# A long convolution beside an FFN in one instruction stream: the second stage's products back come after the next group's spectra, the last stage takes the second half first, and the stages' weights and the casts' places change

## The chip, the cores and the metric

The kernel runs on one core of one Trainium2 chip. The metric is device time of one execution in microseconds. Engines are named as in the profile: PE (matmuls), PEld (its weight loads), DVE, ACT, POOL, and SP, which only issues DMAs; a q behind a name is that engine's instruction queue.

## What is computed

x = A_q has 2048 rows of 576. The output is a sum of three terms:

```python
xn = _layernorm(x, axis=-1)
return x + _A_ref(xn, A_k, A_v, ...) + _B_ref(xn, B_w1, B_w2)
...
# _B_ref: the FFN
h = jnp.maximum(jnp.einsum("bsd,df->bsf", x, w1), 0)
return jnp.einsum("bsf,fd->bsd", h, w2)      # d = 576, f = 4608
...
# _A_ref: q = xn, a short causal convolution of k (4 taps), times v,
# then a causal convolution over all 2048 rows per channel with ssm_k (by FFT),
# plus kv * ssm_D, and a gate with q
return q * y
```

All is float32. The kernel splits operands into a high and a low part of 12 bits each (type fp32r) and multiplies hi x hi, hi x lo and lo x hi.

## The kernel before, in words

**The FFN.** x stands in 16 row tiles of 128 (T = 16), in four blocks b of four tiles. A first half of the work takes blocks 0 and 1 through all of w1 and w2, a second half blocks 2 and 3. w1 and w2 are cut into 12 chunks of 384 columns (three column tiles j), so the chunk index ci runs from 0 to 23. `mm1` (L304) makes one column tile of the hidden layer for a block: 14 matmuls of 512 columns into a PSUM tile psh (two buffers), then ACT makes hh (relu) and DVE ll (the rest). `mm2` (L323) makes one row tile's sum in two halves h of 288 columns: nine matmuls each into pso (three buffers), then DVE adds it to acc, times rstd (L337). `drain` places the mm2 of the last block between the mm1 of the next. Per block that is 42 matmuls of L314 and 72 of L334.

**Weights.** `load_w1` and `load_w2` bring a chunk on SP (one buffer each, r1 and r2). `split_w1` and `split_w2` cast a column tile to hi on ACT (L289, L297) and POOL subtracts for lo (L262). SPLITS says behind which mm1 each stands.

**Layer norm.** `stats` gives mean and variance on DVE, `inv_std` 1/sqrt through ACT's square root. `first_xT` and `make_xT` (L237) centre x, transpose it on PE and split it. They only centre; rstd multiplies at the accumulation, which is allowed since relu commutes with a positive factor. Block 2 and 3 are prepared while chunk 11 runs, in place (L745).

**The convolution** is a generator, `conv` (L379), that yields after each small step. It goes through: loading kt = ssm_k (16 DMAs of small pieces, L392), the first transform of k (wk, 128 matmuls), that of the gated convolution of k and v, called x here (wx, 128 matmuls, with DVE's taps L454 to L463), the second stage (L504 on: 32 groups g, 6 steps and 18 matmuls each) and the last stage (L592 on: 16 tiles t with two units u of two halves; 64 steps of two matmuls, then gate and sum on DVE). Between stages the data goes through DRAM (zk, zx, zy).

**How the two are interleaved.** `tick` (L685) is called twice per mm1 and twice per mm2 with the columns done; it adds `rate` times that to an account, and when the account is not negative it takes one step of the generator and subtracts that step's weight (W_FK, W_FX, W_FM, W_FO, L53). So a larger weight spreads a stage over more of the FFN. A negative yield is a pause in FFN columns. The rate comes from SHARE, the part of the FFN in which the stream is to end. In the last chunk of each half, `mm2` calls `rest_of_stream` at each tile t >= HT = 8 (L342), which takes all steps that are left, because the last sum of those tiles (acc) must contain the convolution. Tiles below 8 were stored to fin in DRAM after the first half, and the last stage reads them back (ft) and stores the result from POOL's queue.

The program is then ordered by the scheduler of the tile framework, which moves an instruction ahead when it expects it to be ready; `tc.issue_after(ins)` keeps instructions behind ins on its engine. So the order on an engine is not the order of the code.

Of the kernel before, what the change touches and what calls it, by code (L numbers as in the profile page):

```python
# [10 lines left out]
F32 = mybir.dt.float32  # L11
# [29 lines left out]
N_WARM = 22  # L41

# [6 lines left out]
SHARE = 0.95  # L49
# [3 lines left out]
W_FK, W_FX, W_FM, W_FO = 1.6, 3.7, 1.8, 2.1  # L53
# [54 lines left out]
def h3_ffn_kernel(ctx: ExitStack, tc, x, k, v, shift_k, ssm_k, ssm_D, w1, w2, fwd, inv, mid, out):  # L108
# [100 lines left out]
    def first_xT(srcs):  # L209
# [7 lines left out]
        for t in range(BT):  # L217
# [3 lines left out]
            with tc.issue_after(behind.ins) if behind else nullcontext():  # L221
                stats(t, srcs[t])
                if t % 2 == 0:
                    behind = nc.vector.tensor_scalar(neg[:, t:t + 1], mv[:, t, 0:1], -1.0, None,
                                                     op0=OP.mult)
                    nc.scalar.activation(xn, srcs[t], AF.Identity, bias=neg[:, t:t + 1])
                else:
                    behind = centred(xn, srcs[t], t)
            for c in range(5):
                w = min(P, D - c * P)  # L230
                nc.tensor.transpose(ps[c][:w, t * P:(t + 1) * P], xn[:, c * P:c * P + w], ident)
        for c in range(5):
            split_x(0, c, ps[c])
# [3 lines left out]
    def make_xT(b, srcs, in_place=False):  # L237
# [3 lines left out]
        with tc.issue_after(done["dve"].ins):  # L241
# [4 lines left out]
        for t in range(t0, t0 + BT):  # L246
# [6 lines left out]
            centred(xn[-1], srcs[t], t)  # L253
        for c in range(5):
# [4 lines left out]
            split_x(b, c, ps)  # L259

# [23 lines left out]
    def split_w1(ci, j):  # L284
# [4 lines left out]
        nc.scalar.activation(h1, r1[:, :, cols], AF.Copy)  # L289
# [3 lines left out]
    def split_w2(ci, j):  # L293
# [3 lines left out]
        nc.scalar.activation(h2, r2[:, j, :], AF.Copy)  # L297
# [4 lines left out]
    hid = {}  # L302

# [19 lines left out]
    def mm2(ci, b, i):  # L323
        t = b * BT + i
        cols = slice(i * P, (i + 1) * P)
        for h in range(2):
# [3 lines left out]
            for j in range(FT):  # L330
# [6 lines left out]
            done["acc"] = nc.vector.scalar_tensor_tensor(  # L337
                acc[t][:, dc], ps[:, :NH], rstd[:, t:t + 1], acc[t][:, dc],
                op0=OP.mult, op1=OP.add)
            tick(W_MM2 / 2)  # L340
        if ci % NCHUNK == NCHUNK - 1:
            if t >= HT:  # L342
                rest_of_stream()
# [3 lines left out]
            else:  # L347
                if t >= T - 2:
                    move(acc[t], out, t, store=True)
                elif t % 2:  # L350
# [28 lines left out]
    def conv():  # L379
# [124 lines left out]
        with tc.tile_pool(name="fm", bufs=2) as fp:  # L504
# [38 lines left out]
            pend = None  # L543
            for g in range(NG + 1):
                yy = None
# [3 lines left out]
                if pend is not None:  # L549
                    yh = fp.tile([P, D], F32R, tag="yh", name=f"yh{g - 1}")  # L550
                    yl = fp.tile([P, D], F32R, tag="yl", name=f"yl{g - 1}")
                    yy = yh, yl
                for h in range(2):
# [6 lines left out]
                    if pend is not None:  # L560
                        if h == 0:
                            p1, p2 = pend
                            nc.vector.tensor_tensor(p1, p1, p2, OP.add)
                            nc.scalar.activation(yh, p1, AF.Copy)
                        else:
                            nc.vector.tensor_tensor(yl, p1, yh, OP.subtract)
                    yield W_FM
                if yy is not None:
                    vo = fp.tile([P, D], F32, tag="vo", name=f"vo{g - 1}")
                for h, (name, z) in enumerate((("k", zk), ("x", zx))):  # L570
                    if yy is not None:
                        ps, cols = run(*yy, 1, h)
                        nc.scalar.activation(vo[:, cols], ps, AF.Copy)
                    split(name, g + 1)
                    load(z, g + 2, name)
                    yield W_FM
                if yy is not None:
                    nc.sync.dma_start(rows(zy, g - 1), vo)
                if g < NG:
                    sw = fp.tile([P, D], F32, tag="sw", name=f"sw{g}", bufs=1)  # L580
                    for h in range(2):
# [4 lines left out]
                        if h == 1:  # L586
                            nc.vector.tensor_tensor(k2, sw, k2, OP.mult)
                        yield W_FM
                    pend = k1, k2


        with tc.tile_pool(name="fo", bufs=2) as fp:  # L592
            raw, parts, rest, ys = {}, {}, {}, {}

            def load_z(t, u):
                if t < T:
                    raw[t, u] = fp.tile([P, D], F32, tag="zt", name=f"zo{t}_{u}", bufs=4)
                    nc.sync.dma_start(raw[t, u], zy[:, T * u + t, :])

            def load_rest(t):  # L600
                if t < T:
# [8 lines left out]
                    rest[t] = w, xt, ft  # L610

            def split(t, u):
                if t < T:
                    hi = fp.tile([P, D], F32R, tag="hi", name=f"ohi{t}_{u}", bufs=3)
                    lo = fp.tile([P, D], F32R, tag="lo", name=f"olo{t}_{u}", bufs=3)
                    with here():
                        nc.scalar.activation(hi, raw[t, u], AF.Copy)
                        nc.vector.tensor_tensor(lo, raw[t, u], hi, OP.subtract)
                    parts[t, u] = hi, lo

            def gate(t):

                if t >= 0:
                    with here():
                        nc.vector.scalar_tensor_tensor(ys[t], rest[t][1], mv[:, t, 0:1], ys[t],
                                                       op0=OP.subtract, op1=OP.mult)

            def add(t):
                if t >= 0:
                    to, more = (ys[t], rest[t][2]) if t < HT else (acc[t], acc[t])  # L630
                    with here():
                        nc.vector.scalar_tensor_tensor(to, ys[t], rstd[:, t:t + 1], more,
                                                       op0=OP.mult, op1=OP.add)
                    if t < HT:
                        move(to, out, t, store=True, queues=(nc.gpsimd, nc.gpsimd))

            units = [(t, u) for t in range(T) for u in range(U)]
            for n in range(3):
                load_z(*units[n])
            for t in range(2):  # L640
# [158 lines left out]
```

## Time and profile before

| | us |
|---|---|
| runs, median of 3 (lowest to highest) | 1116.33 (1114.97 to 1117.08) |
| the profiled execution | 1114.96 |
| its span, first to last instruction | 1113.2 |
| PE, DVE, ACT, POOL busy in it | 1080.5, 737.3, 583.5, 265.4 |

How to read the rows that follow: a group's row has line, engine, operation, out<-in, shapes and count, then busy time in us and mean ns of one, then the engine's idle time just before these instructions and what ended most of it. A timeline row has start and length in us, and in brackets the idle time before it. Busy time on PE counts from a matmul's start to its modelled end, and matmuls overlap; what they really take is seen from start to start.

### The profile page before, as it was taken

What the parts mean: (1) busy time and instruction counts of PE and PEld (TensorE: products, weight loads), DVE (VectorE), ACT (ScalarE), POOL (GpSimd) and SP (SyncE); (2) the same over time, 40 slices, a digit from 0 to 9 for tenths busy, and PEclk for the clock granted to TensorE, in tenths of its full rate; (3) what the DMA queues carried; (4) which work ended last, traced back from release to release, by engine and by line L of the source; (5) the groups of instructions that cost most, each with busy time, mean ns of one, the idle gap of its engine ahead of it and who ended that gap; (6) DMA issues with size and microseconds to landing.
All of it is one profiled execution on the core that took longest, in us unless ns stands there. A gap on an engine that the chain in (4) does not pass through costs nothing.

```text
span 1113.2 us, 17349 instructions
## 1 busy us (share of the span) xinstructions
PE 1080.5 (97%) x6534; PEld 980.5 (88%) x6534; DVE 737.3 (66%) x1215; ACT 583.5 (52%) x1180; POOL 265.4 (24%) x215
## 2 busy tenths in 40 slices
PE   8999999999999999999999999999999999998698
PEld 5889999988898988999989999999999999997587
DVE  6353876759999999358555654655555655468985
ACT  4221778713433343357566665676656666545540
POOL 3230331412412313303121131220312302214200
PEclk9999999999999999999999999999999999999699
DMA  9940464664544533426544133342342412288823
GB/s 236 175 144 1 145 192 138 191 184 140 178 145 152 180 118 130 142 75 201 175 132 132 54 122 99 96 121 64 121 123 63 131 54 90 89 247 248 232 73 86
DMA packets 112640, 150.79 MB, mean 135 GB/s; under 512 B 45229, under 2 KB 63279, under 8 KB 112556
## 3 DMA queue, kind: packets, MB, share of 16 engines
q1 hardware_dynamic: 104572, 135.98, 41.2%
q0 software_dynamic: 7824, 13.11, 4.5%
q8 instruction: 51, 0.84, 0.3%
q10 hardware_dynamic: 160, 0.59, 0.2%
q14 instruction: 33, 0.27, 0.1%
HBM read 114.26 MB, written 35.39 MB: 134 GB/s over the span
## 4 chain that ended last, share of the span: by engine, by line
PE 69%; DVE 16%; DMA 6%; issue 4%; ACT 3%; SPq 1%; POOL 1%; DVEq 0%; ACTq 0%; POOLq 0%
PE pso L334 30%; PE psh L314 29%; PE psf L533 6%; DVE e L457 4%; DVE acc L337 3%; DVE c L458 3%; DMA r<-in_w 2%; PE psf L369 2%; DVE ll L320 1%; DVE xs L363 1%; DVE c L454 1%; SPq L392 1%; DVE c L463 1%; DMA k-1_2411<-in_k 1%; POOL l L262 1%
## 5 line engine op out<-in xcount | busy, mean ns | idle before, releaser
L262 POOL TENSOR_TENSOR l<-r,h 128x640 fp32r<-128x640 f32 (+1 forms) x144 | 229.5, 1609 | 646.6 <-ACT h L297 318.7
L334 PE MATMUL pso<-h,hh 128*128 128x288 f32 x1152 | 339.0, 296 | 7.9 <-DVE acc L337 7.6
L334 PE MATMUL pso<-l,hh 128*128 128x288 f32 x1152 | 339.2, 295 | 0.0
L334 PE MATMUL pso<-h,ll 128*128 128x288 f32 x1152 | 338.9, 295 | 0.0
L337 DVE SCALAR_TENSOR_TENSOR acc<-pso,rstd,acc 128x288 f32<-128x288 f32 x384 | 193.4, 512 | 90.1 <-PE pso L334 88.3
L334 PEld LDWEIGHTS pso<-h,hh 128*128 128x128 f32 x1152 | 216.3, 188 | 17.4 <-DVE acc L337 11.3
L314 PE MATMUL psh<-xhi,h 128*128 128x512 f32 x576 | 226.7, 394 | 1.5 <-DVE ll L320 1.1
L314 PE MATMUL psh<-xlo,h 128*128 128x512 f32 x576 | 226.2, 393 | 0.0
L314 PE MATMUL psh<-xhi,l 128*128 128x512 f32 x576 | 225.6, 392 | 0.0
L334 PEld LDWEIGHTS pso<-l,hh 128*128 128x128 f32 x1152 | 216.8, 188 | 5.3
L334 PEld LDWEIGHTS pso<-h,ll 128*128 128x128 f32 x1152 | 216.7, 188 | 0.7
L320 DVE SCALAR_TENSOR_TENSOR ll<-psh,hh 128x512 fp32r<-128x512 f32 x144 | 98.6, 686 | 123.2 <-ACT hh L319 122.9
L319 ACT ACTIVATE hh<-psh 128x512 fp32r<-128x512 f32 x144 | 85.1, 593 | 141.4 <-PE psh L314 139.8
L314 PEld LDWEIGHTS psh<-xhi,l 128*128 128x128 f32 x576 | 108.5, 188 | 21.7
L314 PEld LDWEIGHTS psh<-xhi,h 128*128 128x128 f32 x576 | 108.3, 188 | 18.4 <-DVE ll L320 1.6
L314 PEld LDWEIGHTS psh<-xlo,h 128*128 128x128 f32 x576 | 108.5, 188 | 15.9 <-DVE xlo L203 0.4
L289 ACT ACTIVATE h<-r 128x640 fp32r<-128x640 f32 x72 | 52.4, 734 | 62.8 <-PE psh L314 30.4
L297 ACT ACTIVATE h<-r 128x576 fp32r<-128x576 f32 x72 | 46.9, 678 | 52.7 <-DMA r<-in_w 29.1
L585 DVE TENSOR_TENSOR k<-psf,k 128x288 f32<-128x288 f32 x64 | 29.1, 455 | 66.8 <-ACT sw L584 66.6
L583 ACT ACTIVATE sw<-psf 64x288 f32<-64x288 f32 x64 | 26.1, 408 | 88.9 <-PE psf L533 87.7
L314 PE MATMUL psh<-xhl,l 128*128 128x512 f32 x144 | 56.5, 392 | 0.0
L314 PE MATMUL psh<-xhl,h 128*128 128x512 f32 x144 | 56.2, 391 | 0.0
(104 smaller groups left out, 1414.3 us busy)
## 6 DMA issues: line engine op xcount, KB each, us to landing
r<-in_w SPq DMA_DIRECT2D x24, 864.0 KB, 6.6
r<-in_w SPq DMA_DIRECT2D x23, 768.0 KB, 5.6
zk<-zk SPq DMA_DIRECT2D x32, 288.0 KB, 2.4
zx<-zx SPq DMA_DIRECT2D x32, 288.0 KB, 2.4
ztk<-zk SPq DMA_DIRECT2D x32, 288.0 KB, 2.8
ztx<-zx SPq DMA_DIRECT2D x32, 288.0 KB, 2.8
zy<-vo SPq DMA_DIRECT2D x32, 288.0 KB, 2.2
zo<-zy SPq DMA_DIRECT2D x32, 288.0 KB, 3.5
```

Source lines behind the costliest of these rows:

```text
L262: return nc.gpsimd.tensor_tensor(dst, src, hi, OP.subtract)
L289: nc.scalar.activation(h1, r1[:, :, cols], AF.Copy)
L297: nc.scalar.activation(h2, r2[:, j, :], AF.Copy)
L314: nc.tensor.matmul(ps, a, m, start=i == 0, stop=i == len(seq) - 1)
L319: done["act"] = nc.scalar.activation(hh, ps, AF.Relu)
L320: nc.vector.scalar_tensor_tensor(ll, ps, 0.0, hh, op0=OP.max, op1=OP.subtract)
L334: nc.tensor.matmul(ps[:, :NH], a[:, cols], m[:, dc], start=n == 0, stop=n == 3 * FT - 1)
L337: done["acc"] = nc.vector.scalar_tensor_tensor(acc[t][:, dc], ps[:, :NH], rstd[:, t:t + 1], acc[t][:, dc], op0=OP.mult, op1=OP.add)
L457: nc.vector.tensor_tensor(e, win[t - n], sk[:, n, :], OP.mult)
L458: nc.vector.tensor_tensor(sums[t], sums[t], e, OP.add)
L533: nc.tensor.matmul(ps[:, :NH], a, m[:, cols], start=n == 0, stop=n == 2)
L585: nc.vector.tensor_tensor(k1[:, cols], ps, k1[:, cols], OP.mult)
```

## The change

- Second stage: in a group the steps of x's spectrum come right behind those of k's. The matmuls back of the group before (run(*back, 1, h)) come last. The sum k1 + k2 and its cast yh are made at the end of their own group, yl at the start of the next one.
- Last stage: tiles 8 to 15 first, then 0 to 7. `rest_of_stream` is no longer called in `mm2`; instead the last chunk's mm2 of tile t takes steps until t is in `added`.
- Stage weights and SHARE are new.
- `make_xT` multiplies by rstd (normalized), so for blocks 1 to 3 DVE's accumulation is a plain add; block 0 keeps the old form. For blocks 2 and 3 the statistics stand behind the last acc instead of the last split of x.
- `at_turn`: from chunk 1 on, the casts of weights on ACT stand behind the last hh.
- Start: tile 3 is centred on ACT too; 6, 3 and 2 more warm matmuls after the transposes of tiles 1, 2 and 3; the warm matmuls write a psh tile; the casts of chunk 0's w1 tiles 1 and 2 stand behind the centring and behind the split of x.
- End: the last tile's store goes out by halves, one part on SP, one on ACT.

```diff
-SHARE = 0.95
+SHARE = 0.985
-W_FK, W_FX, W_FM, W_FO = 1.6, 3.7, 1.8, 2.1
+W_FK, W_FX, W_FM, W_FO = 1.4, 4.1, 1.26, 2.4
...
+            keep_warm(WARM_TILE[t])
+        with tc.issue_after(done["act"].ins):
+            split_w1(0, 1)
...
-        with tc.issue_after(done["dve"].ins):
+        with tc.issue_after(done["acc" if in_place else "dve"].ins):
...
-            centred(xn[-1], srcs[t], t)
+            normalized(xn[-1], srcs[t], t)
...
+    def at_turn(ci):
+        return tc.issue_after(done["act"].ins) if ci else nullcontext()
...
+        if ci == HALVES * NCHUNK - 1:
+            while t not in added:
+                next(stream)
...
+            if b == 0:
+                done["acc"] = nc.vector.scalar_tensor_tensor(
+                    acc[t][:, dc], ps[:, :NH], rstd[:, t:t + 1], acc[t][:, dc],
+                    op0=OP.mult, op1=OP.add)
+            else:
+                done["acc"] = nc.vector.tensor_tensor(acc[t][:, dc], ps[:, :NH], acc[t][:, dc],
+                                                      OP.add)
+            if ci == HALVES * NCHUNK - 1 and t == T - 1:
+                for u, queue in ((0, nc.sync), (1, nc.scalar)):
+                    queue.dma_start(out[u, :, t, dc], acc[t][halves(u)[0], dc])
             tick(W_MM2 / 2)
         if ci % NCHUNK == NCHUNK - 1:
-            if t >= HT:
-                rest_of_stream()
...
+                    for h in range(2):
+                        ps, cols = run(*parts["x", g], 0, h)
+                        nc.scalar.activation(sw[:64, cols], ps[64:], AF.Copy)
+                        nc.scalar.activation(sw[64:, cols], ps[:64], AF.Copy)
+                        nc.vector.tensor_tensor(k1[:, cols], ps, k1[:, cols], OP.mult)
+                        if h == 0:
+                            split("k", g + 1)
+                            load(zk, g + 2, "k")
+                        yield W_FM
...
+                    if back is not None:
+                        ps, cols = run(*back, 1, h)
+                        nc.scalar.activation(vo[:, cols], ps, AF.Copy)
+                    if g < NG:
+                        if h == 0:
+                            nc.vector.tensor_tensor(k2, sw, k2, OP.mult)
+                            split("x", g + 1)
+                            load(zx, g + 2, "x")
+                        else:
+                            nc.vector.tensor_tensor(k1, k1, k2, OP.add)
+                            yh = fp.tile([P, D], F32R, tag="yh", name=f"yh{g}")
+                            nc.scalar.activation(yh, k1, AF.Copy)
+                            pend = yh, k1
...
+            order = [*range(HT, T), *range(HT)]
+            units = [(t, u) for t in order for u in range(U)]
```

Three places in the built program show what moved. In names, the numbers behind a tile's name are chunk, block or tile, and tile half; the last is the buffer's own.

PE in the last stage of the kernel before; ohi and olo are the two parts of a unit's input (tile and unit in the name):

```order
L657 MATMUL psf_10856<-ohi7_0_10788,wi7_10655 128x288
L658 MATMUL psf_10856<-olo7_0_10789,wi7_10655 128x288
L657 MATMUL psf_10894<-ohi7_1_10843,wi7_10655 128x288
L658 MATMUL psf_10894<-olo7_1_10844,wi7_10655 128x288
L657 MATMUL psf_10917<-ohi7_1_10843,wi7_10655 128x288
L658 MATMUL psf_10917<-olo7_1_10844,wi7_10655 128x288
```

and in the changed one, where ohi's number counts the units:

```order
L326 MATMUL psh22_2_0_11194<-xhi2_5203,h1_22_0_10837 128x512
L691 MATMUL psf_11202<-ohi18_11108,wi1_10941 128x288
L692 MATMUL psf_11202<-olo18_11109,wi1_10941 128x288
L326 MATMUL psh22_2_0_11194<-xlo2_5204,h1_22_0_10837 128x512
L326 MATMUL psh22_2_0_11194<-xhi2_5203,l1_22_0_10838 128x512
L326 MATMUL psh22_2_0_11194<-xhi2_5203,h1_22_0_10837 128x512
```

Before, 22 steps of two matmuls each follow one another without an FFN matmul between. Now only pairs or threes stand so, among the stage's first 20 steps, where the mean distance is 11 matmuls; from there to the end it is 17.

SP at the start, before; r1_1 and r2_1 are chunk 1's w1 and w2, kt is ssm_k:

```order
L388 DMA skip_336<-in_ssm_D 1x288 x2
L392 DMA kt_335<-in_ssm_k 64x36x32 x2
L272 DMA r1_1_220<-in_w1 128x4x384
L274 DMA r1_1_220<-in_w1 64x384 x2
L392 DMA kt_335<-in_ssm_k 64x36x32 x5
L281 DMA r2_1_236<-in_w2 128x3x576
L392 DMA kt_335<-in_ssm_k 64x36x32 x9
```

and in the changed kernel:

```order
L408 DMA skip_348<-in_ssm_D 1x288 x2
L412 DMA kt_347<-in_ssm_k 64x36x32 x9
L281 DMA r1_1_232<-in_w1 128x4x384
L283 DMA r1_1_232<-in_w1 64x384 x2
L412 DMA kt_347<-in_ssm_k 64x36x32 x4
L290 DMA r2_1_248<-in_w2 128x3x576
L412 DMA kt_347<-in_ssm_k 64x36x32 x3
```

Chunk 1's w1 stands behind nine loads of kt instead of two, its w2 behind thirteen instead of seven.

DVE's statistics of block 2 (xn8 is its first pair of tiles), before; pso0_4 is chunk 0's sum of tile 4:

```order
L337 SCALAR_TENSOR_TENSOR acc4_214<-pso0_4_0_569,rstd_84,acc4_214 128x288
L337 SCALAR_TENSOR_TENSOR acc4_214<-pso0_4_1_581,rstd_84,acc4_214 128x288
L167 BN_STATS bn8_5356<-xn8_5079 128x6 x2
L167 BN_STATS bn9_5360<-xn8_5079 128x6 x2
L168 BN_AGGR mv_83<-bn8_5356 128x2
L320 SCALAR_TENSOR_TENSOR ll1_0_1_609<-psh1_0_1_592,hh1_0_1_608 128x512
```

and in the changed kernel; pso10_7 is chunk 10's sum of tile 7:

```order
L383 TENSOR_TENSOR xs15_1_5185<-c15_5027,xs15_1_5185 64x576
L357 TENSOR_TENSOR acc6_229<-pso10_7_1_5188,acc6_229 128x288
L168 BN_STATS bn8_5206<-xn8_4999 128x6 x2
L168 BN_STATS bn9_5210<-xn8_4999 128x6 x2
L168 BN_STATS bn10_5214<-xn10_5002 128x6 x2
```

They moved from chunk 0 to the end of chunk 10.

## What the change does to the time: the prediction

> **What bounds the kernel now.** The page comes first: how long, and which engine is busy.
>
> ```profile
> span 1113.2 us, 17349 instructions
> PE 1080.5 (97%) x6534; PEld 980.5 (88%) x6534; DVE 737.3 (66%) x1215; ACT 583.5 (52%) x1180; POOL 265.4 (24%) x215
> PEclk9999999999999999999999999999999999999699
> ```
>
> PE is busy for 1080.5 of 1113.2 us, so 32.7 us are open idle time. The clock row drops near the end, so some busy time there is slow time as well. The windows by stage say where; columns are the stretch, its length, then busy time (and instructions) of PE, PEld, DVE, ACT and POOL, the granted clock, DMA share and GB/s.
>
> ```profile
> 0.00:20.00 20.00, 16.72 (x62) 9.74 (x63) 12.53 (x30) 9.35 (x16) 9.02 (x12) 0.91 0.95 227
> 60.00:80.00 20.00, 17.60 (x104) 15.63 (x103) 13.20 (x31) 5.82 (x10) 7.70 (x6) 1.00 0.47 146
> 120.00:200.00 80.00, 79.95 (x499) 73.62 (x498) 60.69 (x92) 66.56 (x120) 20.60 (x22) 1.00 0.49 150
> 226.00:460.00 234.00, 228.81 (x1379) 207.31 (x1378) 204.01 (x284) 83.07 (x159) 61.56 (x48) 1.00 0.48 147
> 475.00:976.00 501.00, 500.30 (x3106) 461.28 (x3105) 284.21 (x495) 320.19 (x685) 103.18 (x66) 1.00 0.35 108
> 983.00:1085.00 102.00, 86.86 (x478) 75.85 (x477) 90.80 (x155) 51.15 (x107) 21.91 (x33) 0.90 0.68 200
> 1020.00:1060.00 40.00, 27.16 (x123) 22.11 (x121) 36.95 (x65) 22.25 (x48) 9.87 (x18) 0.74 0.83 242
> ```
>
> The row 120 to 200 lies in the first transform of k, 226 to 460 is the one of x, 475 to 976 the second stage, 983 to 1085 the last stage. PE has no idle time worth the name in the first and the third of these; it loses 5.2 us in x's stage, where DVE is at 87%, and 15.1 us in the last one, where DVE is at 89% and at 92% in its middle. The groups of that middle name the wait:
>
> ```profile
> L657 PE MATMUL psf<-ohi,wi 128*128 128x288 f32 x33 | 13.9, 426 | 12.8 <-DVE y L660 12.8
> L660 DVE TENSOR_TENSOR y<-psf,low 64x288 f32<-64x288 f32 x31 | 14.1, 454 | 1.2 <-ACT low L659 0.5
> ```
>
> PE waits for DVE's y, which frees the PSUM buffer. So two things bound the kernel: PE almost everywhere, and DVE where a transform's work is packed too closely.
>
> For the slow time I need PE's step from one matmul to the next, out of the timeline:
>
> ```profile
> 850.50 0.29 PE L334 MATMUL pso<-h,hh 128*128 128x288 f32 x1
> 850.63 0.30 PE L334 MATMUL pso<-l,hh 128*128 128x288 f32 x1
> 851.36 0.39 PE L314 MATMUL psh<-xhi,l 128*128 128x512 f32 x1
> 851.59 0.39 PE L314 MATMUL psh<-xhi,h 128*128 128x512 f32 x1
> ```
>
> A 288-column matmul takes 0.132 us, one of 512 columns 0.228 us (durations overlap; starts count).
>
> **The last stage, the largest term.** In the order of before, 140 matmuls of L314, 203 of L334 and its own 128 stand between the stage's first and last: 140 x 0.228 + 331 x 0.132 = 75.6 us of PE. The stage takes 102 us. So 26 us are lost there, 15.1 idle and the rest at the lower clock. The reason is in the order: 22 of its 64 steps follow each other with nothing between, since L343 pulls the rest of the stream at the first tile of the second half. In the changed order 308 of L326 and 514 of L349 lie between: 308 x 0.228 + 642 x 0.132 = 155 us. DVE's own part of the stage: 90.8 less 10 ll and 22.6 acc of the FFN. Their means:
>
> ```profile
> L337 DVE SCALAR_TENSOR_TENSOR acc<-pso,rstd,acc 128x288 f32<-128x288 f32 x174 | 88.0, 512 | 44.1 <-PE pso L334 44.1
> L320 DVE SCALAR_TENSOR_TENSOR ll<-psh,hh 128x512 fp32r<-128x512 f32 x66 | 45.3, 686 | 60.9 <-ACT hh L319 60.8
> L585 DVE TENSOR_TENSOR k<-psf,k 128x288 f32<-128x288 f32 x64 | 29.1, 455 | 66.8 <-ACT sw L584 66.6
> ```
>
> So 90.8 - 10 x 0.686 - 22.6 x 0.512 = 72.4 us. In 155 us it meets 22 ll and 57 acc, the latter now at 455 ns, the row of the nearest plain add: 72.4 + 15.1 + 26 = 113.4 us, or 73%. At 76% (row 120 to 200) PE lost 0.05 us; at 87% (x's stage) 2.2%. Nearest is the first; since the loads of a half with ft are denser I leave 2.5 us of loss: **-23.5** (bounds -17, if it loses 6% of the 155 us, between the 2% of x's stage and the 15% here, and -25.5). The clock goes with the idle time.
>
> **x's stage.** The stretch grows: 550 and 945 FFN matmuls between its first and last instead of 392 and 684, about 70 us more. DVE's own part stays, 204 less 33 ll and 88 acc, 136 us; with 44 ll, 117 acc and an estimated 20 us for preparing blocks 2 and 3 it is 240 in 299 us, 80%. Of 5.2 us I keep 1.5: **-3.7** (0 to -5.2).
>
> **The second stage** pays for both. Its FFN share falls from 907 and 1539 matmuls to 599 and 1019: 599 x 0.228 + 1595 x 0.132 = 347 us instead of 494. The moved steps are the same in number; yh is cast half a group before its matmuls, which is the cover for yl. ACT decides here. Its FFN work in the old window, and yh:
>
> ```profile
> L319 ACT ACTIVATE hh<-psh 128x512 fp32r<-128x512 f32 x66 | 39.3, 595 | 55.7 <-PE psh L314 54.6
> L289 ACT ACTIVATE h<-r 128x640 fp32r<-128x640 f32 x33 | 24.1, 731 | 15.8 <-PE psh L314 10.3 <-PE pso L334 3.1 <-DMA r<-in_w 2.4
> L297 ACT ACTIVATE h<-r 128x576 fp32r<-128x576 f32 x33 | 21.3, 675 | 6.7 <-DMA r<-in_w 4.0 <-PE pso L334 2.7
> L564 ACT ACTIVATE yh<-k 128x576 fp32r<-128x576 f32 x32 | 21.6, 674 | 0.5 <-DVE q L177 0.3 <-DVE k L563 0.2
> ```
>
> 320.2 - 84.7 = 235.5 us are the stage's own; with 599/907 of 84.7 it is 291 in 349 us, 83%. The row 120 to 200 has ACT at 66.56 of 80, also 83%, without PE idling. But there no cast had to wait for a DVE sum as yh does; I take **+1.5** (0 to +8).
>
> **The early statistics.** DVE stands still for a load that it needs only at chunk 11:
>
> ```profile
> 59.16 1.54 DVE L167 BATCH_NORM_STATS2 bn<-xn 128x6 f32<-128x288 f32 x4 [4.72 <-DMA xn<-in_x]
> ```
>
> That is what PE's 2.4 us idle in 60 to 80 follows. The statistics move behind chunk 10's last acc (L357): **-2.4** (0 to -2.4). At the half boundary they and the longer chain to rstd (six short steps, then the normalised copy) come at once, beside the end of x's stage; twelve transposes wait for them, with 60 matmuls queued in between: **+0.5** (-0.7 to +4).
>
> **The start and chunk 1's weights.** PE, then SP, then ACT:
>
> ```profile
> 11.42 0.55 PE L231 MATMUL psf<-ident,xn 128*128 128x128 f32 x3 [1.25 <-ACT xn L226]
> 15.53 0.63 PE L314 MATMUL psh<-xhi,h 128*128 128x512 f32 x1
> 17.80 0.39 PE L314 MATMUL psh<-xhi,h 128*128 128x512 f32 x1
> 12.47 6.64 SPq L392 DMA_DIRECT2D kt<-in_ssm_k  x2
> 19.23 1.50 SPq L272 DMA_DIRECT2D r<-in_w  x1
> 33.30 1.68 SPq L281 DMA_DIRECT2D r<-in_w  x1
> 35.03 17.65 SPq L392 DMA_DIRECT2D kt<-in_ssm_k  x9
> 39.93 1.26 ACT L297 ACTIVATE h<-r 128x576 fp32r<-128x576 f32 x2 [3.18 <-DMA r<-in_w]
> 41.09 1.06 ACT L319 ACTIVATE hh<-psh 128x512 fp32r<-128x512 f32 x2
> 42.45 0.50 PE L314 MATMUL psh<-xhi,h 128*128 128x512 f32 x1 [0.95 <-DVE ll L320]
> ```
>
> From about 14 to 17.5 us matmuls of 512 columns last 0.63 instead of 0.39 us: half clock, about 1.9 us lost. The change adds 11 warm matmuls against that; the order puts ten ahead of the first transposes (they take 2.2 us, and the transposes of tile 2 had to wait until 11.42 anyway) and one between. [...]
>
> SP now issues nine kt before chunk 1's w1 instead of two, and thirteen before its w2 instead of seven. A kt takes 17.65 / 9 = 1.96 us of the queue, so w2's issue moves from 33.3 to about 45.1, and its landing from 39.9 to about 51.7. Behind it on ACT now stands h2 of chunk 1 and then hh of block 1's third column tile (L308, L331): 51.7 + 0.7 + 0.6 = 53.0. In before the work that precedes its reader, 28 matmuls of each size after 42.45, was done at 42.45 + 28 x 0.228 + 28 x 0.132 = 52.5; without the 0.95 us wait PE would be there at 51.5, and at full clock from the start at 49.6. It waits either way. Net 53.0 - 52.5 = **+0.5** (-1.9 if the queue is quicker and the clock holds, +4 if w2 lands at 55).
>
> **The end and the rest.** The tail begins with the last sum, and SP issues two stores for it one after the other:
>
> ```profile
> 1108.60 0.52 DVE L337 SCALAR_TENSOR_TENSOR acc<-pso,rstd,acc 128x288 f32<-128x288 f32 x1 [0.67 <-PE pso L334]
> 1106.77 3.48 SPq L151 DMA_DIRECT2D out<-acc  x4
> ```
>
> From 1108.60 to the end are 4.6 us. The last store now goes out in halves, one on SP and one on ACT; one issue in four of 3.48 us, less a little, is saved: **-0.6** (0 to -1). The plain add takes 57 ns less on 288 of 384 sums, the weight casts stand at their turn, a centring goes from DVE to ACT, the warm tile moves to psh: off the path, at nothing; PE's own work covers them, and a DVE or ACT above its limit is in the stage terms already.
>
> **Sum.** -23.5 - 3.7 + 1.5 - 2.4 + 0.5 + 0.5 - 0.6 = -27.7 us. The profiled execution took 1114.96 us (span 1113.2 and 1.8 around it), so 1087.3; the median of the runs shown, 1116.33, is 1.4 higher than it, and I forecast **1088**, between the two. A measurement of this kernel can tell 0.2% (about 2.2 us) from no change.
>
> **The rivals.**
> - *The last stage stays half bound by DVE.* y, olo, gate and sum come in bursts, and its first third is still packed (11 matmuls from step to step, later 17); a mean of 73% hides that. For it: x's stage loses 2.2% at 87%. Half of 23.5 comes back: 1100. Chance 0.10.
> - *The weights stay late.* Chunk 1's w1 and w2 land after 42 and 52, and the wait passes on to chunk 2's loads, one buffer each. For it: DMA share 0.95 in the first 20 us. Against: chunk 2's w1 stands behind the same sixteen kt in both orders. As much again as w2's delay of 11.8 us, less the 4 to 6 us that a chunk's casts can hide: 6 to 8 us more, 1095. Chance 0.10.
> - *ACT bounds the second stage, and the kernel gets slower.* A group has 349 / 32 = 10.9 us, ACT's work in it is 9.1. If ACT, in its fixed order, waits over 1.8 us per group for DVE's sum before yh, PE stretches; from 1.8 + 27.7 / 32 = 2.7 us on, the whole gain is gone; at 2.8 it is 1114.96 + 32 x 0.1 = 1118. Against: in before yh waits 0.5 us in all. Chance 0.05.
> - *All losses go.* 1078 to 1081. Chance 0.05.
> - The forecast, 1081 to 1094: 0.70. That the change does not do what it says is excluded by the order for the stages; only the warm matmuls are not where the code has them.
>
> Range 1080 to 1102: it takes in both milder rivals and the bounds of start and boundary, not the slower rival. Faster 0.94 (all but that rival and a gain eaten to within 0.2%), same 0.01, slower 0.05.
>
> **What would show it.** Right: last stage of about 155 us with DVE near 73%, no drop of the clock there, PE idle under 3 us; second stage about 350 us with ACT near 83% and PE busy throughout; x's stage under 2 us idle; no wait of DVE for xn near 59 us; a wait of PE for hh at 50 to 54 us behind w2. Wrong: PE waiting for ACT's copies between 530 and 880 us, or for y after 880.

## The result and the profile after

The changed kernel takes **1087.4 us** (median of 4 runs, 1083.8 to 1087.9), the kernel before 1115.7 beside it: ratio 0.974, 95% interval 0.971 to 0.976. The forecast was 1088. The total is right; the terms below it are less so.

The page of the profiled execution (1087.86 us):

```profile
span 1086.1 us, 17315 instructions
PE 1071.6 (99%) x6545; PEld 977.4 (90%) x6545; DVE 730.9 (67%) x1215; ACT 584.9 (54%) x1181; POOL 260.5 (24%) x215
PEclk9989999999999999999999999999999999999999
L357 DVE TENSOR_TENSOR acc<-pso,acc 128x288 f32<-128x288 f32 x288 | 128.9, 452 | 71.6 <-PE pso L349 68.6
```

The windows by stage, with the columns of the prediction. 226 to 526 is x's stage, 545 to 898 the second one, 908 to 1063 the last:

```profile
0.00:20.00 20.00, 18.51 (x81) 11.00 (x81) 11.44 (x31) 10.44 (x18) 8.24 (x12) 1.00 0.95 229
50.00:60.00 10.00, 6.10 (x22) 5.20 (x21) 2.20 (x4) 2.23 (x4) 2.79 (x2) 0.66 1.08 233
60.00:80.00 20.00, 20.00 (x119) 18.08 (x119) 5.58 (x11) 4.69 (x8) 6.14 (x4) 1.00 0.43 120
226.00:526.00 300.00, 299.64 (x1817) 273.58 (x1816) 234.89 (x373) 103.47 (x191) 76.25 (x59) 1.00 0.47 141
545.00:898.00 353.00, 349.23 (x2185) 322.24 (x2184) 229.57 (x381) 285.87 (x629) 69.32 (x44) 1.00 0.37 118
908.00:1063.00 155.00, 155.00 (x946) 142.03 (x945) 113.82 (x201) 67.28 (x134) 43.40 (x44) 1.00 0.51 152
```

The last stage takes 155 us with PE never idle, DVE at 113.8 / 155 = 73% and the full clock: every figure of that step came out. x's stage has 0.4 us idle, DVE at 78%. The second stage has ACT at 81% and 3.8 us idle. New is the hole at 50 to 60 us: 3.9 us idle, clock 0.66.

Idle time and slow time together are told by **PE's loss**: over all matmuls, the step to the next start less the matmul's own step (as in the traces of before and after: 0.2275 us for 512 columns, 0.132 for 288, 0.110 for a transpose; nothing for a warm one, which so counts as lost in full). What is left without loss is 1051 us, the same in every kernel, since apart from the warm ones all hold the same matmuls. Losses of the profiled executions in us, by place (start = to 38 us; w2 = 38 to 62; stats = 62 us to the transform of k; a stage's column runs from its first matmul to the first of the next stage; tail = from the last matmul's start), with the kernels of the experiments:

| | start | w2 | stats | k | x | second | last | tail | span |
|---|---|---|---|---|---|---|---|---|---|
| before | 12.7 | 1.3 | 3.0 | 2.2 | 7.3 | 4.1 | 26.4 | 4.9 | 1113.2 |
| after | 11.8 | 6.7 | 0.3 | 1.5 | 1.6 | 7.7 | 1.0 | 4.1 | 1086.1 |
| e0_after_again | 12.5 | 5.4 | 0.3 | 1.5 | 1.6 | 7.5 | 1.0 | 4.1 | 1085.2 |
| e1_stage_times_only | 12.5 | 2.7 | 2.5 | 3.0 | 5.4 | 17.7 | 45.1 | 4.9 | 1145.2 |
| e2_old_stage_times | 12.7 | 5.2 | 0.3 | 1.8 | 1.3 | 4.2 | 1.2 | 4.1 | 1082.1 |
| e3_old_second_stage | 12.0 | 5.4 | 0.3 | 1.5 | 1.6 | 50.4 | 15.9 | 4.1 | 1142.6 |
| e4_weights_ahead | 12.3 | 0.0 | 1.7 | 2.0 | 1.6 | 4.6 | 1.0 | 4.1 | 1078.7 |
| e5_no_extra_warm | 12.9 | 0.1 | 1.5 | 1.9 | 1.6 | 5.3 | 1.0 | 4.1 | 1079.8 |
| e6_early_stats | 12.5 | 0.0 | 7.3 | 1.5 | 1.6 | 4.7 | 1.0 | 4.1 | 1084.2 |
| e7_old_sums | 13.0 | 1.2 | 2.1 | 1.7 | 3.3 | 5.0 | 2.0 | 4.2 | 1083.8 |
| e8_second_stage_only | 12.7 | 1.6 | 2.7 | 3.1 | 6.8 | 6.5 | 1.1 | 4.9 | 1091.0 |
| e9_both | 12.5 | 0.0 | 2.2 | 1.5 | 1.3 | 4.8 | 1.2 | 4.1 | 1079.0 |
| e10_split_after_hh | 12.2 | 0.0 | 4.9 | 1.5 | 1.6 | 5.0 | 1.0 | 4.1 | 1081.7 |
| e12_no_turn | 12.4 | 5.0 | 0.3 | 2.3 | 2.8 | 4.6 | 1.1 | 4.1 | 1084.0 |

25.4 of the 27.1 us between the spans came from the last stage. x's stage and the statistics gave 8.4 more, the start, k's stage and the tail 2.4; the wait for w2 and the second stage took 9.0 back (0.1 is rounding).

The hole at 50 us in the timeline of after, ACT then PE, and the loads ahead of it on SP's queue:

```profile
53.42 0.68 ACT L308 ACTIVATE h<-r 128x576 fp32r<-128x576 f32 x1 [7.73 <-DMA r<-in_w]
54.01 0.58 ACT L331 ACTIVATE hh<-psh 128x512 fp32r<-128x512 f32 x1
54.65 0.61 PE L349 MATMUL pso<-h,hh 128*128 128x288 f32 x1 [3.90 <-ACT hh L331]
```

```profile
11.80 22.19 SPq L412 DMA_DIRECT2D kt<-in_ssm_k  x9
34.12 1.39 SPq L281 DMA_DIRECT2D r<-in_w  x1
36.74 9.59 SPq L412 DMA_DIRECT2D kt<-in_ssm_k  x4
46.43 1.53 SPq L290 DMA_DIRECT2D r<-in_w  x1
```

A kt takes 22.19 / 9 = 2.47 us of the queue, not the 1.96 of the row used. w2 is issued at 46.4 and its cast starts at 53.4 (forecast 45.1 and 51.7). The windows show what followed, in stretches of 3.41 us:

```profile
49.80:53.21 3.41, 0.95 (x8) 0.72 (x6) 0.00 (x0) 0.00 (x0) 0.00 (x0) 1.00 1.16 307
53.21:56.62 3.41, 1.97 (x8) 1.98 (x9) 1.63 (x3) 2.23 (x4) 2.44 (x2) 0.50 1.06 169
56.62:60.04 3.42, 3.42 (x10) 2.75 (x9) 0.58 (x2) 0.00 (x0) 0.36 (x1) 0.50 1.02 235
60.04:63.45 3.41, 3.41 (x22) 3.10 (x22) 1.06 (x2) 0.60 (x1) 0.00 (x0) 1.00 1.02 255
```

After the stretch in which PE was busy 0.95 of 3.41 us, the granted clock is half for the next two. The wait of 3.9 us so grew to 6.7 lost.

### The profile page after: what moved, and what is told of

Same layout as the page of the kernel before. It is cut to its first block, busy times and chain, and to the rows that moved or that the text cites. A ratio compares the mean times of both kernels' runs of the same rounds, so it can differ in the third digit from the quotient of the medians.

```text
span 1086.1 us, 17315 instructions
## 1 busy us (share of the span) xinstructions
PE 1071.6 (99%) x6545; PEld 977.4 (90%) x6545; DVE 730.9 (67%) x1215; ACT 584.9 (54%) x1181; POOL 260.5 (24%) x215
## 4 chain that ended last, share of the span: by engine, by line
PE 89%; DMA 5%; SPq 2%; DVE 2%; ACT 1%; issue 1%; POOL 0%; ACTq 0%; DVEq 0%
PE pso L349 39%; PE psh L326 38%; PE psf L553 6%; DMA r<-in_w 3%; PE psf L389 3%; SPq L412 2%; PE psf L691 1%; PE psf L692 1%; DMA k-1_2423<-in_k 1%; DMA acc<-in_x 0%; DMA sk<-in_shift_k 0%; PE psf L263 0%; DVE lox L544 0%; DVE lok L544 0%; DVE acc L357 0%
## 5 line engine op out<-in xcount | busy, mean ns | idle before, releaser
L271 POOL TENSOR_TENSOR l<-r,h 128x640 fp32r<-128x640 f32 (+1 forms) x144 | 224.4, 1562 | 625.0 <-ACT h L299 448.8
L357 DVE TENSOR_TENSOR acc<-pso,acc 128x288 f32<-128x288 f32 x288 | 128.9, 452 | 71.6 <-PE pso L349 68.6
L353 DVE SCALAR_TENSOR_TENSOR acc<-pso,rstd,acc 128x288 f32<-128x288 f32 x96 | 48.2, 513 | 31.1 <-PE pso L349 30.5
L383 DVE TENSOR_TENSOR ks<-kt,ks 64x288 fp32r<-64x288 f32 x64 | 57.6, 900 | 2.0
L390 ACT ACTIVATE zx<-psf 128x288 f32<-128x288 f32 x64 | 25.8, 407 | 59.2 <-PE psf L389 38.5
```

The lines of the kernel that those rows point to most:

```text
L271: return nc.gpsimd.tensor_tensor(dst, src, hi, OP.subtract)
L353: done["acc"] = nc.vector.scalar_tensor_tensor(acc[t][:, dc], ps[:, :NH], rstd[:, t:t + 1], acc[t][:, dc], op0=OP.mult, op1=OP.add)
L357: done["acc"] = nc.vector.tensor_tensor(acc[t][:, dc], ps[:, :NH], acc[t][:, dc], OP.add)
L383: nc.vector.tensor_tensor(dst[other], src[own], dst[own], OP.subtract)
```

## The experiments

Times are medians; ratios are to the kernel before run beside them (1118.4 to 1119.9 us in these runs). The runs form three sets, each on its own chip: e1 to e4; e5 and e7 to e9; e0, e6, e10 and e12. Between sets, 2 or 3 us are at the edge of what can be told apart.

**The changed kernel again**, so that the others can be compared with it.

> The changed kernel once more, beside the next three. Theory: the kernel before took 1119 to 1120 us beside the other experiments, against 1115.7 beside the first run of the changed kernel, so the ratios to it are comparable only by a run here. The changed kernel takes 1086 to 1090; with the old stage times, at 1084.0, 2 to 4 us are still gained, since the changed kernel loses 4 us at the start and in the middle of the second stage that the old times don't lose. Rival (the difference lay between chips): 1084 or less here.

Measured 1087.2 us, ratio 0.972 (0.970 to 0.974): as the theory has it. That is 31 us below the kernel before run beside it; in the first measurement it was 28.

**Only the numbers**, in the kernel before:

```diff
-SHARE = 0.95
+SHARE = 0.985
-W_FK, W_FX, W_FM, W_FO = 1.6, 3.7, 1.8, 2.1
+W_FK, W_FX, W_FM, W_FO = 1.4, 4.1, 1.26, 2.4
```

> The kernel before with only the two lines of numbers changed (the four stage times and the share). Theory (the last stage gains because its steps are pulled one tile at a time, and the new numbers need that): the rest of the stream is still pulled at the first tile of the second half, and in the order only 42 and 141 FFN matmuls now lie inside the last stage, 45 us of PE beside 72.4 us of DVE's own work, 41 of the first 42 steps with nothing between. The last stage takes about 90 us and loses 40 to 45 us instead of 26; x's stage, with 527 and 900 matmuls inside, loses 1 to 2 us less than 5.2 before. Time 1122 to 1132 us, slower than before. Rival (the numbers carry the gain): last stage near PE's own speed, 1090 to 1100 us.

Measured 1144.6 us, ratio 1.023 (1.020 to 1.025): slower, and 13 us above the range that I expected. Its windows, second and last stage:

```profile
545.00:1020.00 475.00, 471.62 (x2903) 433.36 (x2901) 259.60 (x441) 307.63 (x659) 96.21 (x62) 1.00 0.32 99
1032.00:1120.00 88.00, 63.89 (x301) 52.76 (x300) 78.92 (x140) 45.97 (x97) 17.35 (x30) 0.69 0.75 223
```

The last stage lost 45 us, as said. Missed: 17.7 us lost in the second stage's column (4.1 before), 11.7 of them after 1000 us, where its last steps stand bare of FFN work too and PE then waits 7.6 us for a load of what it left in DRAM (zo). From its first matmul to its last that stage still takes 482 us (494 before) though its number is 30% smaller. So, in this order, the numbers hardly set its length.

**The old numbers** in the changed kernel (the diff above, reversed).

> The changed kernel with the four stage times and the share of before. Theory: what fills the last stage is the pull by tile, not the numbers: 252 and 459 FFN matmuls lie inside it, 135 us of PE, DVE near 80%, so it loses 1 to 2 us; x's stage is as packed as before (392 and 684 matmuls) and loses 3 to 5 us; the second stage has 394 us of PE and loses less than 2. Time 1090 to 1093 us, 3 to 5 above the changed kernel. Rival (the numbers carry the gain): the last stage loses 10 us or more, 1100 or above.

Measured 1084.0 us, ratio 0.969 (0.966 to 0.971): not slower than the changed kernel but some 3 us faster, at the edge of what the intervals tell apart.

```profile
226.00:450.00 224.00, 223.35 (x1357) 204.10 (x1356) 193.31 (x283) 84.40 (x159) 62.37 (x48) 1.00 0.50 152
894.00:1028.00 134.00, 134.00 (x828) 123.26 (x827) 109.33 (x191) 64.63 (x130) 42.20 (x43) 1.00 0.59 172
```

The last stage loses nothing in 134 us with DVE at 82%. And x's stage, as packed as before and with DVE at 86%, idles 0.65 us: my theory that a DVE near 87% costs PE 2% there falls.

**The old second stage** in the changed kernel (the function's loop over g as in the kernel before).

> The changed kernel with the second stage's order of before (matmuls back between k's and x's spectra). Theory: at the new pace the old order is too slow in the second stage, the order gives the last stage's first 20 steps nearly nothing between them (about 112 FFN matmuls, 18 us of PE, for 23 us of DVE), so the last stage loses 5 to 8 us and the time is 1092 to 1096. Rival (the new order of the second stage costs, since the cast of yh waits 35 us for DVE's sum in all): without it PE loses less in the second stage and the time is 1082 to 1086.

Measured 1146.0 us, ratio 1.024 (1.021 to 1.027). Both theories named far too little: this one part is worth 59 us. The groups of the second stage tell how many groups went by (hix has four matmuls in a group); e3 in 545 to 900 us, then after in 545 to 898:

```profile
L553 PE MATMUL psf<-hix,m_sb 128*128 128x288 f32 x102 | 29.0, 297 | 0.4 <-ACT hix L543 0.4
```

```profile
L553 PE MATMUL psf<-hix,m_sb 128*128 128x288 f32 x128 | 36.1, 297 | 1.9 <-ACT hix L543 1.9
```

25.5 groups in 355 us are 13.9 us each; the new order has 32 in 353, 11.0 each. In the traces a group of the old order holds about 70 FFN matmuls there (62 to 78), one of the new order about 50, with the same numbers. PE was busy in both. The groups that the old order had not done by then come at the end, bare; window, and PE's waits of the whole run:

```profile
920.00:975.00 55.00, 29.79 (x115) 24.62 (x113) 22.45 (x36) 37.22 (x87) 0.00 (x0) 0.58 0.15 49
```

```profile
PE psf L553 <- ACT yh L586: 22.7, 6, 4.7
```

There a group takes 10 us (5.5 groups in the window), of which PE waits about 4 for yh, and the mean granted clock is 0.58.

**Only the new second stage**, in the kernel before (the other half of the same test):

> The kernel before with only the second stage's order of the changed kernel; numbers, pull at the first tile of the second half, tile order, sums, start and statistics are those of before. Theory now (the second stage's order is what fills the last stage: in the order of before a group can't be laid out in fewer than about 73 FFN matmuls, in the new one it takes about 55, so the stream no longer falls behind and nothing is left to be pulled in a bunch): 252 and 459 FFN matmuls lie in the last stage instead of 140 and 203, it loses 1 to 3 us instead of 26, x's stage and the early statistics lose what they lost. Time 24 to 26 us below the kernel before run beside it. Rival (the pull by tile or the new numbers are needed as well): 10 us below it, or less.

Measured 1098.2 us, ratio 0.981 (0.978 to 0.983): 21.7 us gained, where the whole change gains 28 to 31, with the old numbers, the old pull at the first tile of the second half, the old tile order and the old start.

```profile
226.00:460.00 234.00, 228.17 (x1375) 206.81 (x1374) 203.84 (x284) 82.33 (x158) 61.37 (x47) 1.00 0.48 147
902.00:1036.00 134.00, 134.00 (x828) 123.33 (x827) 108.46 (x192) 65.13 (x130) 43.39 (x47) 1.00 0.60 176
```

The last stage's loss is gone, x's stage idles 5.8 us, about as before. Of the 2 to 4 us short of the expectation, 2.4 are in the second stage (6.5 lost instead of 4.1). The profiled execution was the fastest of five, at 1092.9; what the others lost more is open.

How many FFN matmuls the numbers ask for in a group follows from the code: six steps of W_FM / rate columns each, where a block has 42240 columns and 114 matmuls. That is 59 with the old numbers and 47 with the new ones. The new order comes near it: 60 in e2 and e8, 51 in the changed kernel. The old order does not: in the kernel before and in e1 the groups repeat the same 72, 74 and 82, though the numbers differ.

**The old sums**, on top of the old numbers:

```diff
-            normalized(xn[-1], srcs[t], t)
+            centred(xn[-1], srcs[t], t)
...
-            if b == 0:
-                done["acc"] = nc.vector.scalar_tensor_tensor(
...
-            else:
-                done["acc"] = nc.vector.tensor_tensor(acc[t][:, dc], ps[:, :NH], acc[t][:, dc],
-                                                      OP.add)
+            done["acc"] = nc.vector.scalar_tensor_tensor(
+                acc[t][:, dc], ps[:, :NH], rstd[:, t:t + 1], acc[t][:, dc],
+                op0=OP.mult, op1=OP.add)
```

> The changed kernel with the four stage times and the share of before (the run that took 1084.0), and with the sums of before: accumulators of blocks 1 to 3 are added with rstd in one instruction (512 instead of 452 ns), and these blocks are centred instead of normalised. Theory: x's stage is as packed as before, and what freed it was the plain sum: DVE goes from 86% back to 88% of it and PE loses 3 to 5 us there. Time 1087 to 1089. Rival (4 us of DVE's work don't matter there): no loss, 1084.

Measured 1087.0 us, ratio 0.972 (0.969 to 0.974).

```profile
226.00:450.00 224.00, 222.07 (x1341) 202.04 (x1341) 199.12 (x282) 83.69 (x158) 61.23 (x48) 1.00 0.50 152
```

The time is as expected, the place only in part: x's stage loses 3.3 instead of 1.3, so the plain sum gives 2 of the 6 us that this stage gained with the old numbers. (The wait for w2 was smaller here too, since hh stood ahead of the cast on ACT; that hides part of the cost.)

**The weights ahead of kt:**

```diff
-    load_w2(1)
+    done["r"] = load_w2(1)
...
-        nc.sync.dma_start(r2, w2[f0:f0 + FC, :].rearrange("(j p) d -> p j d", p=P))
         raw_w[2, ci] = r2
+        return nc.sync.dma_start(r2, w2[f0:f0 + FC, :].rearrange("(j p) d -> p j d", p=P))
...
-                    nc.sync.dma_start(kt[halves(h)[0], d:d + KD, :], src)
+                    with tc.issue_after(done["r"].ins) if d else nullcontext():
+                        nc.sync.dma_start(kt[halves(h)[0], d:d + KD, :], src)
```

> The changed kernel with 14 of the 16 loads of kt put behind both loads of chunk 1's weights on SP's queue. Theory: chunk 1's w2 then lands before 35 us instead of 53.4, PE's waits for it between 50 and 60 us (6.6 us lost, the half clock after them included) go, and the granted clock stays at 1.00 there. Nothing else waits for kt before 115 us. Time 1080 to 1082 us, about 6 below the changed kernel. Rival 1 (the late kt push chunk 2's loads back and the wait moves there): 1085 to 1088. Rival 2 (the clock falls there for another reason than the wait): the wait goes, but the clock stays at half between 53 and 60 us, 1084.

Measured **1081.2 us**, ratio 0.966 (0.964 to 0.968), the lowest median of all; window, then ACT's timeline:

```profile
40.00:60.00 20.00, 20.00 (x115) 17.86 (x115) 6.66 (x12) 5.70 (x10) 7.46 (x5) 1.00 1.04 183
```

```profile
42.65 0.68 ACT L308 ACTIVATE h<-r 128x576 fp32r<-128x576 f32 x1
...
65.01 0.74 ACT L299 ACTIVATE h<-r 128x640 fp32r<-128x640 f32 x1 [8.89 <-DMA r<-in_w]
```

The cast of w2 waits for no load, PE is busy throughout, the clock stays at 1.00. Part of rival 1 is true: 1.7 us are now lost behind chunk 2's w1, which comes at 65 us.

**Only the cast's place:**

```diff
-SPLITS0 = {(1, 0): ((1, 0), (1, 1)), (1, 1): ((1, 2), (2, 0)), (1, 2): ((2, 1), (2, 2))}
+SPLITS0 = {(1, 0): ((1, 0), (1, 1)), (1, 1): ((1, 2),), (1, 2): ((2, 0), (2, 1), (2, 2))}
```

> The changed kernel with one split moved: h2 of chunk 1's first column tile stands behind hh of block 1's third column tile on ACT instead of ahead of it; SP's order and the landing of w2 near 53 us stay. Theory (PE does not need w2 near 50 us; it waits because hh is queued on ACT behind a cast that waits for w2): PE's wait near 50 us and the half clock after it go though w2 lands as late, the loss between 38 and 62 us falls from 6.7 to under 2. Time 4 to 5 us below the changed kernel run beside it. Rival (w2's landing itself is needed): no change.

Measured 1084.2 us, ratio 0.970 (0.968 to 0.973), 3.0 us below the changed kernel instead of 4 to 5. The cast of w2 starts at 52.4, about as late as in after, and between 38 and 62 us nothing is lost: PE waited for what was queued on ACT, not for w2. But the same pattern stands one chunk on, where h of chunk 2's w1 is ahead of hh; ACT, then PE:

```profile
66.44 0.74 ACT L299 ACTIVATE h<-r 128x640 fp32r<-128x640 f32 x1 [10.50 <-DMA r<-in_w]
67.08 0.58 ACT L331 ACTIVATE hh<-psh 128x512 fp32r<-128x512 f32 x1
68.80 0.41 PE L349 MATMUL pso<-h,hh 128*128 128x288 f32 x1 [2.75 <-DVE acc L357]
```

The row names acc: on DVE the ll of that hh comes first (67.69 us), and the sums behind it (from 68.30) free the pso that PE needs. 4.9 us are lost there, so of the 3.0 gained only 1 to 2 are near the start; the rest is in the second stage.

**Both gains** (e4's edit and the old numbers):

> The changed kernel with both edits that gained: the four stage times and the share of before, and 14 of the 16 loads of kt behind both loads of chunk 1's weights. Theory: the two gains are in different places (the start of the second stage and its middle, 4 us; the wait for w2 near 53 us, 5 us) and add up: 1077 to 1079. Rival (one of them was a difference between chips): 1081 or above.

Measured 1083.2 us, ratio 0.968 (0.966 to 0.971): they don't add up. The table says why: about 3 of the 3.5 us that the changed kernel loses more than e2 in the second stage are not lost in e4 and e10 either. In the changed kernel that loss begins like the one at 50 us: on ACT hix, which the stage's first matmuls need, stands behind a cast that waits for a w2.

```profile
546.48 0.69 ACT L308 ACTIVATE h<-r 128x576 fp32r<-128x576 f32 x1 [7.27 <-DMA r<-in_w]
548.12 0.67 ACT L543 ACTIVATE hix<-ztx 128x576 fp32r<-128x576 f32 x1
```

That load takes 11.0 us from issue to landing, where the median of the changed kernel's 24 loads of w2 is 5.1; in e10, with the same loads in the same order around it, PE doesn't wait. Why it takes so long in the changed kernel is open. The wait near 50 us alone is not enough: e3 and e12 lose 5 us there too, and in them PE hardly waits at the second stage's start.

**No extra warm matmuls** (WARM_TILE all zero):

> The changed kernel without the eleven warm matmuls among the first transposes (which compute nothing that is used). Theory: the granted clock goes by PE's busy share in stretches of 3.41 us, transposes counted; with gaps of over 1 us between the first transposes one stretch falls to about half or less, the clock is at half for 3.41 us from about 12 to 15 us, and the first 512-column matmuls lose 1.7 us. That is hidden by the wait for chunk 1's w2: PE's wait near 50 us gets shorter by as much, the time stays within 1 us of the changed kernel. Rival 1: the clock stays at full, the warm matmuls were not needed. Rival 2: the loss passes through, 2 us longer.

Measured 1084.6 us, ratio 0.969 (0.966 to 0.971). The clock fell, to 0.50 from 10.90 to 17.73 us (rows in the last section), two stretches of 3.41 us where the theory has one; that transposes count in the busy share rests on e1 alone (there too). The rest was otherwise: the order on SP changed with it.

```profile
12.40 17.79 SPq L412 DMA_DIRECT2D kt<-in_ssm_k  x7
30.32 1.53 SPq L281 DMA_DIRECT2D r<-in_w  x1
33.08 6.48 SPq L412 DMA_DIRECT2D kt<-in_ssm_k  x3
39.66 1.45 SPq L290 DMA_DIRECT2D r<-in_w  x1
```

With ten kt instead of thirteen ahead of it w2 comes 7 us sooner and the hole at 50 us is gone. So this run doesn't test the absorption. By the table the warm matmuls save 0.4 to 1.1 us up to 38 us, and cost 4 to 5 (columns w2 and stats together) by what they do to SP's order.

**The statistics at their old place**, on top of e4:

```diff
-        with tc.issue_after(done["acc" if in_place else "dve"].ins):
+        with tc.issue_after(done["dve"].ins):
```

> The kernel with the weights ahead of kt (1081.2), with the statistics of the second half at their old place. Theory: DVE waits for xn near 59 us again, and PE loses 2 to 3 us between 62 us and the first transform instead of the 1.7 that it loses there waiting for chunk 2's w1; since both waits lie at the same place they overlap, and the time grows by about 1 us, not by the 2.4 that the prediction took. Rival (they add up): 2.4 us or more.

Measured 1083.9 us, ratio 0.970 (0.967 to 0.972): 2.7 us slower by the medians, as the rival has it. DVE's wait:

```profile
59.96 1.54 DVE L168 BATCH_NORM_STATS2 bn<-xn 128x6 f32<-128x288 f32 x4 [6.97 <-DMA xn<-in_x]
```

In the profiled execution 5.6 us more are lost there.

**Without the edges for the casts** (`at_turn` returns nullcontext() always):

> The changed kernel without the edges that hold a chunk's weight casts at their turn on ACT (my prediction put those at nothing). In the order the casts of chunk 1's w1 now stand ahead of hh of block 1's first column tile, which was behind them. Theory: at the start hh waits for w1's landing near 43 us instead of 39, so the loss between 38 and 62 us grows by 3 to 5 us; in x's stage, where the kernel with old sums and no such edges lost 6.8 us and the one with old sums and the edges 3.3, the loss grows from 0.8 to 2 or 3. Time 5 to 7 us above the changed kernel run beside it. Rival (the edges are worth nothing, as predicted): within 1 us.

Measured 1086.0 us, ratio 0.971 (0.969 to 0.973), 1.2 us below the changed kernel, so near the rival. x's stage does lose 2.8 instead of 1.6, but at the start PE only waits at another place (3.2 us up to 46.8, for hh behind chunk 1's w1, and no longer for w2), and the second stage loses less.

## Why the prediction was right, and where it was not

- **Last stage, -23.5.** Measured -25.4, just inside the bound; length, DVE's share and clock as worked out. The counts of matmuls in the built program carried it. The cause I gave failed, though: "The reason is in the order: 22 of its 64 steps follow each other with nothing between, since L343 pulls the rest of the stream at the first tile of the second half." e8 keeps that pull and loses nothing. The pull found so much left because the old second stage was never laid out in less than about 14 us a group; e1 and e3 show that neither numbers nor the pull by tile help then. With the new order the groups keep near the numbers and little is left to pull. Why the old layout stops there was not tried: the chain from the sum over yh to the matmuls back, inside one group, may be it.
- **"The second stage pays for both", +1.5.** Measured +3.6. PE's waits in it, then ACT's group of yh in 545 to 898 us, both of after:

```profile
PE psf L553 <- ACT hix L543: 1.9, 1, 1.9
PE psf L553 <- DVE k L589: 1.2, 2, 0.6
```

```profile
L608 ACT ACTIVATE yh<-k 128x576 fp32r<-128x576 f32 x32 | 22.0, 686 | 35.1 <-DVE k L606 35.0
```

  The first wait is at the stage's first matmuls, behind the late w2 shown with e9; the second is near 650 and 695 us. ACT at 81% did not bound the stage; yh waited 35.0 / 32 = 1.1 us a group for the sum, under the 1.8 that I had as the limit. And the new order is no price: it is what gave most of the gain.
- **x's stage, -3.7 (0 to -5.2).** Measured -5.7, beyond the bound, which was idle time alone (that fell by 4.8). The rule by DVE's share failed: at 86% in e2 PE idled 0.65 us. So did what I built on it, the longer stretch: e2 has the old stretch and loses 1.3, the changed kernel 1.6, so the length gave nothing. The plain sum, which I priced at nothing, is worth 2 us here, and the casts' turn, also at nothing, about 1; some 2.5 us are not accounted for.
- **Early statistics, -2.4.** Measured -2.7; e6 finds 2.7 by the medians.
- **Start and chunk 1's weights, +0.5 (-1.9 to +4).** Mis-sized, and past its bound: -0.9 up to 38 us and +5.4 at w2, +4.5 in all. The chain was right down to the instruction (w2, then h2, then hh on ACT, PE behind it). Two things were too small: a kt at 1.96 us of the queue instead of 2.47 (the row of the first two in the kernel before, 6.64 / 2 = 3.32, spoke against it), and the half clock that followed the wait, for 6.83 us from 53.21 on, which I had not counted. e4 takes the term away.
- **End, -0.6.** Measured -0.8. **Half boundary, +0.5:** nothing there.

That the sum of -27.7 met -27.1 (spans) so closely is luck: the start and the second stage, 6 us worse than said, were made up by x's stage, the last stage and the rest. What was not luck is the last stage, sized from the order alone to within 2 us. Of the rivals, "the weights stay late" was half true: w2's wait is there, and e4 and e10 show that chunk 2's loads are next in line; the 4 to 6 us that a chunk's casts can hide, which its price used, stand in no row.

## What to carry to other kernels

In this kernel a stage's length is set by its weight only as long as its own dependent steps can be laid out that tightly; a weight that asks for less than that moves the surplus to the end, where it stands bare. Before a change is credited to its numbers or its code, try each alone: here the numbers alone cost 25 us, one loop's order alone gave 22, and the whole 28 to 31. And look at what is queued behind the first reader of a late load: in e10 the cast of w2 began at 52.4 us, in after at 53.4, and the loss between 38 and 62 us was 0.0 against 6.7.

## What the runs showed of the hardware

**In these traces the granted clock changes on a grid of 3.41 us.** It is half from 53.21 to 60.04 us in after and, in the kernel before, from 14.05 to 17.47 and from 1031.22 to 1051.70: two, one and six stretches of 3.41 us. In e10 a stretch that was busy 1.55 of 3.41 us, with 1.86 us of the wait of 2.75 in it, was followed by half clock; in e0 one that was busy 1.52:

```profile
66.94:70.35 3.41, 1.55 (x11) 1.50 (x11) 1.82 (x5) 2.03 (x4) 3.08 (x3) 1.00 0.02 5
70.35:73.76 3.41, 3.41 (x11) 2.83 (x10) 0.42 (x1) 0.63 (x2) 1.40 (x1) 0.50 0.24 28
```

```profile
546.14:549.55 3.41, 1.52 (x6) 0.81 (x5) 2.90 (x4) 3.38 (x8) 2.77 (x2) 1.00 1.07 227
549.55:552.96 3.41, 3.38 (x14) 3.38 (x15) 1.70 (x3) 3.27 (x8) 0.00 (x0) 0.50 0.92 254
```

Near half busy both outcomes stand in the kernel before: a stretch with 1.80 us busy (from 10.63) was followed by half clock, one with 1.78 (from 389.52) by full clock.

```profile
10.63:14.05 3.42, 1.80 (x11) 1.26 (x12) 2.23 (x4) 2.90 (x6) 2.90 (x2) 1.00 1.07 344
14.05:17.47 3.42, 3.42 (x9) 2.42 (x9) 3.36 (x6) 3.32 (x7) 2.89 (x3) 0.50 1.03 232
389.52:392.93 3.41, 1.78 (x11) 1.30 (x10) 2.98 (x4) 3.14 (x7) 1.53 (x2) 1.00 0.38 116
392.93:396.35 3.42, 3.42 (x20) 2.96 (x19) 3.42 (x7) 0.29 (x1) 0.51 (x2) 1.00 0.75 249
```

In after (rows above), the stretch at half clock that was busy 1.97 of 3.41 us was followed by another at half, the one busy 3.42 of 3.42 by full clock.

**In e1 the clock came back after a stretch of transposes.** The start of e1, and the transposes (L231) of its first two stretches alone:

```profile
8.10:11.51 3.41, 1.50 (x10) 1.03 (x10) 3.18 (x11) 1.48 (x3) 0.45 (x1) 1.00 1.11 290
11.51:14.92 3.41, 3.22 (x12) 2.30 (x13) 2.21 (x3) 2.90 (x6) 3.05 (x3) 0.50 1.06 335
14.92:18.33 3.41, 3.41 (x17) 2.87 (x16) 3.35 (x6) 2.99 (x7) 2.79 (x3) 1.00 1.04 225
```

```profile
8.10:11.51 3.41, 1.50 (x10) 1.03 (x10) 1.00 1.11 290
11.51:14.92 3.41, 2.61 (x10) 1.75 (x10) 0.50 1.06 335
```

The first stretch has ten transposes in 1.50 of 3.41 us, and the next one is at half clock. That one is busy 3.22, of which transposes take 2.61, and in the third the clock is back: without the transposes the second was busy 0.61 us, less than the five stretches of the kernel before (1031.22 to 1048.29, busy 1.35 to 2.25) that were at half and were followed by half. In e5 a like stretch with 2.87 busy, 2.39 of it transposes, was followed by another at half:

```profile
10.90:14.31 3.41, 2.87 (x12) 2.40 (x12) 0.88 (x4) 3.08 (x6) 2.99 (x2) 0.50 1.09 348
14.31:17.73 3.42, 3.42 (x10) 2.66 (x9) 3.36 (x6) 3.42 (x7) 1.50 (x1) 0.50 1.02 232
```

In the kernel before, ten transposes are 1.53 of the 1.80 us that the stretch from 10.63 was busy; the half clock follows it. In after the twenty transposes have eleven warm matmuls among them: the stretches from 8.83 and 12.24 are busy 3.41 and 3.16 us, and the clock is 1.00 through the first 20 us. In e5, without the eleven, it is half from 10.90 on, after a stretch busy 1.42. So what went with the fall was the idle time between the transposes, not the transposes themselves.
